# The order of 16 small matmuls in a linear-attention and MLP kernel: two batches by turns, or one after the other

## Chip, cores and metric

The kernel runs on 1 core of one Trainium2 chip. The metric is the device time of the execution in microseconds (us), as the median of several runs. The profile is taken by the hardware profiler from one execution of its own.

## What is computed

Inputs are q, k, v of shape (8 batches, 8 heads, 576 positions, 64) and two weight matrices, 512 x 2048 and 2048 x 512, in float32. For each batch and head:

```
phi(x) = [relu(x) * cos(w), relu(x) * sin(w)]      # 128 features, w by position
kv  = phi(k)^T v          (128 x 64)      z = sum over positions of phi(k)
num = phi(q) kv           (576 x 64)      den = phi(q) z + 1e-06
x   = num / den           -> 4608 tokens x 512
out = relu(x @ w_in)^2 @ w_out            -> 4608 x 512
```

## The kernel before, in words

Everything runs in bfloat16 on TensorE with sums in PSUM. The kernel has two parts that it weaves together: the attention of batch b, and the MLP of batches before it. The MLP's products mostly use a Strassen-like scheme with seven products in place of eight (the tiles ha, hb, hc, ya, yb, yc), and plain products near the start (hps, yh).

A batch has 576 positions: four blocks of 128 and a rest of 64. For each block the numerator (`num_div`, L685) takes 8 matmuls, one a head: the turned query features of the block (`qpT`, 128 features x 128 positions) are the stationary operand, loaded by a weight load, and the head's 65 columns of `kvz` (kv and z side by side, so numerator and denominator come out together) are the moving one. The result, 128 positions x 65 columns a head, goes to the tile `num`: two PSUM banks, four heads in each.

The rests of 64 positions of two successive batches b-1 and b (b odd) are taken together, once a pair. Rows 0 to 63 of `num` are for batch b-1, rows 64 to 127 for batch b (`sides`, by b % 2). This is `mm_num` with j == J (L599), which calls `mm_num_tail` (L610) for the one batch and then for the other. Each call issues 8 matmuls, one a head, whose stationary operand is 128 features x 64 positions. They fill half of the array's columns: 0 to 63 for batch b-1 and 64 to 127 for batch b. The loops run over `hh` (four heads) and `half` (which of the two banks). All 16 are first and last of their sums: nothing accumulates. The turned features of a pair's rests lie in one tile, `qpTt`.

One division by DVE (`div`, L642) then serves both batches: it adds a small constant to the denominators (L627), takes the reciprocal (L628) and multiplies (L633), into `xpt`. There are four such groups of 16, for the pairs (0, 1), (2, 3), (4, 5) and (6, 7). What they yield is turned by a transpose and used by the last step of the MLP (`G8` and `Y8`), which handles the rests of all batches.

The order of work is written out by hand. `Plan` holds operations with their dependencies, and `ORDER` (L23) lists all of them by name; `Plan.run` (L221) walks the list, picks the buffer of each tile with estimated times and emits the instructions, so each engine executes its operations in the order of that list. The four groups are its entries num1.4, num3.4, num5.4 and num7.4, each one indivisible operation for the plan, with an estimated time of 0.5 us on TensorE. Each stands far behind num1.3, num3.3 and so on, the other numerators of the later batch, which read the same `kvz`. All matmuls are issued by `mm` (L460), so the profile shows them under L461; they are told apart by tiles: the 16 of a group are `num<-kvz,qpTt`, and the weight loads (PEld) `<-qpTt`. The other numerators are `num<-kvz,qpT`.

Of the kernel before, what the change touches and what calls it, by code (L numbers as in the profile page):

```python
# [282 lines left out]
def kernel(  # L283
# [13 lines left out]
    E1 = D + 1  # L297
# [6 lines left out]
    HH = H // 2  # L304
# [98 lines left out]
    sides = [slice(g * TAIL, (g + 1) * TAIL) for g in range(2)]  # L403
# [56 lines left out]
    def mm(out, lhsT, rhs, start, stop=True):  # L460
        nc.tensor.matmul(  # L461
            out=out, lhsT=lhsT, rhs=rhs, start=start, stop=stop, skip_group_check=True
        )
# [5 lines left out]
    vs, kq, kqt, fe, fet, kz, kvz, qpT, qpTt = {}, {}, {}, {}, {}, {}, {}, {}, {}  # L469
# [128 lines left out]

    def mm_num(num, b, j):  # L599
        if j == J:  # L600
            for i in range(2):
                mm_num_tail(num, b - 1 + i)
            return
        for hh in range(HH):
            for half in range(2):
                e0, h = hh * E1, half * HH + hh
                o, lhsT = num[half][:, e0 : e0 + E1], qpT[b, j // 2][:, j % 2, h, :]
                mm(o, lhsT, kvz[b][:, h * E1 : (h + 1) * E1], True)

    def mm_num_tail(num, b):  # L610
        for hh in range(HH):
            for half in range(2):
                e0, h, s_ = hh * E1, half * HH + hh, sides[b % 2]
                o = num[half][s_, e0 : e0 + E1]
                lhsT = old_turned(b)[:, hh, sides[half]] if b < 2 else qpTt[b][:, h, s_]
                mm(o, lhsT, kvz[b][:, h * E1 : (h + 1) * E1], True)

    def old_turned(b):
        return qpTt[b][:, b * HH : (b + 1) * HH, :]
# [65 lines left out]
    def num_div(b, j, after, bufs):  # L685
        num = buf("n", [P, 2, FP], F32, "num")
        den = buf("den", [P, 2, 2, HH], F32, "den")
        xbuf = xp[b, j // 2] if j < J else xpt[b]
        n = plan.op(
            f"num{b}.{j}",  # L690
            {"PE": 0.244 if j < J else 0.5},
            lambda e: mm_num([num[:, 0], num[:, 1]], b, j),
            after,
            [num, kvz[b], den, xbuf] + bufs,
        )
        return plan.op(
            f"div{b}.{j}",
            {"DVE": 0.99},
            lambda e: div(num[:, :], b, j, den),
            [n],  # L700
            [num, den, xbuf],
        )
# [919 lines left out]
```

## Time and profile before

| | us |
|---|---|
| median of 3 runs | 272.38 |
| lowest and highest | 271.87, 273.05 |
| the profiled execution, its own time | 271.95 |
| its span, first to last instruction | 269.9 |
| matmuls (PE) busy in it | 263.1 |
| weight loads (PEld) busy | 225.0 |
| DVE, ACT busy | 228.1, 186.7 |

PE is TensorE's matmuls and PEld its weight loads, which overlap with matmuls. Each group of 16 stands in the profile as 16 instructions with 65 columns each (128 features in, 64 positions out). The length given for one instruction (0.19 to 0.22 us here) is the time until it has passed the array; the next one starts well before that, so what an instruction costs is read from the distances between starts. A view by windows counts the instructions that touch a window; if all windows begin before the group, the count is how many have started by the window's end.

### The profile page before, as it was taken

The page shows a single profiled execution, that of the slowest core. Times are in us where ns is not written, and L with a number is a line of the kernel's source. Part 1 is how long each engine was busy: PE and PEld are TensorE (multiplying, and loading weights), DVE is VectorE, ACT ScalarE, POOL GpSimd, SP SyncE. Part 2 cuts the span into 40 slices and gives each one's busy share as a digit, 9 for nine tenths or more (in the row PEclk, how much of TensorE's full clock was granted, in tenths as well). Part 3 has the DMA queues.
Part 4 walks back from the last instruction along what each step waited for, and adds up shares of the span by engine and source line. Part 5 has one row for each costly group of instructions (what it writes and reads, how often), then busy time and mean ns, then how long its engine had stood idle before and what let it go on. Part 6 is the DMA issues. An engine that isn't in the chain of part 4 may idle for free.

```text
span 269.9 us, 6751 instructions
## 1 busy us (share of the span) xinstructions
PE 263.1 (97%) x2787; PEld 225.0 (83%) x2792; DVE 228.1 (85%) x412; ACT 186.7 (69%) x289; POOL 26.9 (10%) x44
## 2 busy tenths in 40 slices
PE   8899999999999999999999999999999999999994
PEld 3568856699899889989998998899888888888883
DVE  3877987889998999999999999899978858797941
ACT  4762695698888997689699868587658636755510
POOL 8934443200000000000000000000000000000000
PEclk9999999999999999999999999999999999999999
DMA  6999999999899999999899998652540111010115
GB/s 221 220 206 253 328 198 250 298 295 298 221 247 314 221 261 298 300 183 231 284 275 209 232 359 208 152 155 100 61 125 15 38 63 78 8 72 2 78 50 186
DMA packets 82367, 51.23 MB, mean 190 GB/s; under 512 B 53217, under 2 KB 78817, under 8 KB 82337
## 3 DMA queue, kind: packets, MB, share of 16 engines
q1 hardware_dynamic: 71008, 38.28, 55.5%
q0 software_dynamic: 10736, 12.00, 21.2%
q10 hardware_dynamic: 592, 0.52, 0.6%
q8 instruction: 22, 0.36, 0.6%
q14 instruction: 9, 0.07, 0.1%
HBM read 36.70 MB, written 9.44 MB: 171 GB/s over the span
## 4 chain that ended last, share of the span: by engine, by line
PE 83%; DMA 12%; POOL 3%; issue 0%; DVE 0%; POOLq 0%
PE ya L461 18%; PE yb L461 16%; PE hb L461 13%; PE ha L461 8%; PE hc L461 8%; PE hps L461 8%; DMA w1sb<-in_moe_w_in_dram 5%; DMA kq<-in_k_dram 4%; PE num L461 3%; DMA w2sb<-in_moe_w_out_dram 3%; PE kz L461 3%; PE yc L461 3%; PE yh L461 3%; POOL kq L509 1%; POOL w1sb L411 1%; POOL v L1378 1%
## 5 line engine op out<-in xcount | busy, mean ns | idle before, releaser
L461 PEld LDWEIGHTS <-w1sb 128*128 128x128 bf16 x736 | 70.4, 98 | 8.6
L461 PEld LDWEIGHTS <-gs 128*128 128x128 bf16 x512 | 49.9, 98 | 5.8
L461 PEld LDWEIGHTS <-gT 128*128 128x128 bf16 x448 | 43.1, 98 | 9.8 <-issue 0.2
L442 ACT ACTIVATE gT<-gT 128x1024 bf16<-128x1024 bf16 x38 | 39.5, 1059 | 3.4 <-DVE gT L455 1.8
L461 PE MATMUL hps<-xT,w1sb 128*128 128x256 bf16 x320 | 37.4, 273 | 0.0
L448 ACT ACTIVATE fe<-kq,cols 128x1024 bf16<-128x1024 f32 (+1 forms) x39 | 35.1, 950 | 2.8 <-DMA kq<-in_k_dram 1.7
L461 PEld LDWEIGHTS <-w1s 128*128 128x128 bf16 x312 | 29.7, 98 | 3.3
L461 PE MATMUL ya<-w2sb,gT 128*128 128x256 bf16 x256 | 30.7, 273 | 0.0
L461 PE MATMUL hb<-xs,w1sb 128*128 128x256 bf16 x208 | 30.6, 273 | 0.0
L450 DVE TENSOR_SCALAR fe<-kq,cols 128x1024 bf16<-128x1024 f32 (+1 forms) x41 | 26.9, 690 | 4.0 <-DMA kq<-in_k_dram 4.0
L461 PE MATMUL ha<-xT,w1sb 128*128 128x256 bf16 x176 | 26.2, 273 | 0.0
L444 DVE TENSOR_TENSOR gT<-gT 128x1024 bf16<-128x1024 bf16 x34 | 23.2, 686 | 1.2 <-ACT gT L436 0.8
L436 ACT ACTIVATE gT<-ha 128x512 bf16<-128x512 f32 x21 | 12.6, 601 | 15.9 <-PE ha L461 15.9
L633 DVE TENSOR_TENSOR xp<-num,den 128x512 bf16<-128x512 f32 (+1 forms) x33 | 22.2, 675 | 1.1
L436 ACT ACTIVATE gT<-hps 128x512 bf16<-128x512 f32 x26 | 15.4, 602 | 8.1 <-PE hps L461 8.0
L455 DVE CUSTOM_DVE_ANT_0 gT<-hb,s 128x512 bf16<-128x512 f32 x26 | 17.8, 686 | 3.7 <-PE hb L461 3.3
L458 DVE TENSOR_TENSOR gs<-gT 128x2048 bf16<-128x2048 bf16 x16 | 19.4, 1219 | 0.4
L455 DVE CUSTOM_DVE_ANT_0 gT<-hc,u 128x512 bf16<-128x512 f32 x26 | 17.7, 683 | 0.8 <-PE hc L461 0.8
L432 ACT COPY hb<-ha 128x512 f32<-128x512 f32 x26 | 15.2, 585 | 4.3 <-DVE gT L438 1.8
L461 PE MATMUL hb<-xs,w1s 128*128 128x256 bf16 x104 | 15.6, 273 | 0.0
L436 ACT ACTIVATE gT<-hb 128x512 bf16<-128x512 f32 x18 | 10.8, 599 | 7.0 <-PE hb L461 4.5
L461 PE MATMUL hc<-xs,w1s 128*128 128x256 bf16 x104 | 15.6, 273 | 0.0
(120 smaller groups left out, 415.7 us busy)
## 6 DMA issues: line engine op xcount, KB each, us to landing
out_dram<-y SPq DMA_DIRECT2D x16, 512.0 KB, 3.7
vs<-in_v_dram SPq DMA_DIRECT2D x10, 512.0 KB, 4.8
kq<-in_k_dram SPq DMA_DIRECT2D x5, 1024.0 KB, 7.1
kq<-in_q_dram SPq DMA_DIRECT2D x5, 1024.0 KB, 9.2
w1sb<-in_moe_w_in_dram POOLq DMA_DIRECT2D x4, 512.0 KB, 11.6
w2sb<-in_moe_w_out_dram POOLq DMA_DIRECT2D x4, 512.0 KB, 10.3
kq<-in_q_dram POOLq DMA_DIRECT2D x2, 1024.0 KB, 11.2
kq<-in_k_dram POOLq DMA_DIRECT2D x2, 1024.0 KB, 11.1
```

What stands on the lines that cost most here:

```text
L411: nc.gpsimd.dma_start(out=w1sb[:, :, f0:f1], in_=moe_w_in[:, f0:f1].rearrange("(kb p) f -> p kb f", p=P),)
L432: (nc.scalar.copy if e == "ACT" else nc.vector.tensor_copy)(out=out, in_=in_)
L436: nc.scalar.activation(out=out, in_=in_, func=ACTF.Relu)
L442: nc.scalar.activation(out=out, in_=in_, func=ACTF.Square)
L444: nc.vector.tensor_tensor(out=out, in0=in_, in1=in_, op=ALU.mult)
L448: nc.scalar.activation(out=out, in_=in_, func=ACTF.Relu, scale=col)
L450: nc.vector.tensor_scalar(out=out, in0=in_, scalar1=0.0, scalar2=col, op0=ALU.max, op1=ALU.mult)
L455: nc.vector._custom_dve(dve_ops.TENSOR_ADD_SAT, out=out, in0=in0, in1=in1, s0=BIG, s1=0.0)
L458: nc.vector.tensor_tensor(out=out, in0=in0, in1=in1, op=op)
L461: nc.tensor.matmul(out=out, lhsT=lhsT, rhs=rhs, start=start, stop=stop, skip_group_check=True)
L509: eng.dma_start(out=kq[b][:, "kq".index(nm)][:, hs, js], in_=main_of(nm, b)[:, hs, js])
L633: nc.vector.tensor_tensor(out=x, in0=n4[:, :, :, 0:D].rearrange("p b (k l) d -> p b k l d", l=2), in1=r.rearrange("p b (k l) -> p b k l", l=2)
```

## The change

The 16 matmuls of a group are issued in another order. Before: all 8 of batch b-1, then all 8 of batch b. After: for each head and bank, the one of batch b-1 and then the one of batch b. `mm_num_tail` becomes the body of the loops, with `hh` and `half` as arguments. Operands, results, and everything else of the kernel are the same, as is `ORDER`.

```diff
     def mm_num(num, b, j):
         if j == J:
-            for i in range(2):
-                mm_num_tail(num, b - 1 + i)
+            for hh in range(HH):
+                for half in range(2):
+                    for i in range(2):
+                        mm_num_tail(num, b - 1 + i, hh, half)
             return
...
-    def mm_num_tail(num, b):
-        for hh in range(HH):
-            for half in range(2):
-                e0, h, s_ = hh * E1, half * HH + hh, sides[b % 2]
-                o = num[half][s_, e0 : e0 + E1]
-                lhsT = old_turned(b)[:, hh, sides[half]] if b < 2 else qpTt[b][:, h, s_]
-                mm(o, lhsT, kvz[b][:, h * E1 : (h + 1) * E1], True)
+    def mm_num_tail(num, b, hh, half):
+        e0, h, s_ = hh * E1, half * HH + hh, sides[b % 2]
+        o = num[half][s_, e0 : e0 + E1]
+        lhsT = old_turned(b)[:, hh, sides[half]] if b < 2 else qpTt[b][:, h, s_]
+        mm(o, lhsT, kvz[b][:, h * E1 : (h + 1) * E1], True)
```

## Prediction

> **What bounds the kernel now.** I read the page first: busy times, the chain that ended last, then the waits of TensorE. From the page:
>
> ```profile
> PE 263.1 (97%) x2787; PEld 225.0 (83%) x2792; DVE 228.1 (85%) x412; ACT 186.7 (69%) x289; POOL 26.9 (10%) x44
> PEclk9999999999999999999999999999999999999999
> PE 83%; DMA 12%; POOL 3%; issue 0%; DVE 0%; POOLq 0%
> ```
>
> TensorE (PE) is busy 97% of a span of 269.9 us at full clock, and it is 83% of the chain that ended last. The 16-matmul bursts that change run at 73, 94, 170 and 210 us, so what counts is whether PE is the bound from 73 us to the end. Two views answer that. The first is the table of busy time by stretch (us of the stretch's length, then busy us and number of instructions of each engine):
>
> ```profile
> 73.00:94.00 21.00, 21.00 (x258) 18.82 (x256) 19.30 (x38) 18.76 (x28) 0.00 (x0) 1.00 1.04 251
> 94.00:170.00 76.00, 76.00 (x865) 68.34 (x864) 73.60 (x133) 63.11 (x97) 0.00 (x0) 1.00 1.06 258
> 170.00:211.00 41.00, 41.00 (x450) 36.82 (x451) 35.62 (x63) 27.17 (x42) 0.00 (x0) 1.00 0.38 91
> 211.00:264.00 53.00, 53.00 (x487) 47.43 (x486) 40.22 (x58) 27.31 (x44) 0.00 (x0) 1.00 0.15 53
> ```
>
> PE's busy time equals the length of each stretch. The second is the view of waits: all of PE's own, then those of its weight loads from 50 to 265 us, then the longest of all engines from 73.6 to 260 us (first and fourth of that answer).
>
> ```profile
> PE wm L461 <- DVE zeros L362: 1.2, 1, 1.2
> PE tq L1428 <- DVE fe L450: 0.7, 1, 0.7
> PE num L461 <- ACT kvz L432: 0.2, 1, 0.2
> ```
> ```profile
> PEld L461 <- issue: 0.8, 4, 0.2
> ```
> ```profile
> ACT gT L436 <- PE ha L461: 15.9, 11, 3.5
> ...
> ACT u L432 <- PE hb L461: 3.6, 7, 1.0
> ```
>
> PE's three waits belong to the warm-up and the first batch. In the stretch that matters its weight loads stand still 4 times for 0.2 us, and on nothing that the profile names: those are the starts of the four bursts. The other engines wait for PE, not the reverse. So in this stretch every tenth of a microsecond that PE is spared should come off the end, and every tenth that it is given should be added.
>
> **What the bursts cost now.** Of each burst, the chart of instructions in order of time (start, length, engine, work, count) shows the burst and what follows. All four, each from its own answer:
>
> ```profile
> 72.59 0.60 PE L461 MATMUL yc<-w2t,gs 128*128 128x256 bf16 x4
> 73.12 0.60 PE L461 MATMUL num<-kvz,qpTt 128*64 128x65 bf16 x16
> 73.65 0.61 PE L461 MATMUL yb<-w2t,gs 128*128 128x256 bf16 x4
> ```
> ```profile
> 94.14 0.60 PE L461 MATMUL num<-kvz,qpTt 128*64 128x65 bf16 x16
> 94.67 0.50 PE L461 MATMUL ya<-w2sb,gT 128*128 128x256 bf16 x3
> ```
> ```profile
> 169.90 0.60 PE L461 MATMUL num<-kvz,qpTt 128*64 128x65 bf16 x16
> 170.43 0.61 PE L461 MATMUL hb<-xs,w1sb 128*128 128x256 bf16 x4
> ```
> ```profile
> 210.27 0.60 PE L461 MATMUL num<-kvz,qpTt 128*64 128x65 bf16 x16
> 210.80 0.61 PE L461 MATMUL hb<-xs,w1sb 128*128 128x256 bf16 x4
> ```
>
> From the first matmul of a burst to the first of the next work it is 0.53 us in all four. The inside of a burst is read from windows that all begin at 73.10 and end later and later: the count behind PE is how many of the 16 have started by then, the count behind PEld how many weight loads have.
>
> ```profile
> 73.10:73.13 0.03, 0.01 (x1) 0.01 (x1) 0.00 (x0) 0.00 (x0) 1.00 0.00 0
> 73.10:73.17 0.07, 0.05 (x1) 0.05 (x2) 0.00 (x0) 0.00 (x0) 1.00 0.56 59
> 73.10:73.18 0.08, 0.06 (x2) 0.06 (x3) 0.00 (x0) 0.00 (x0) 1.00 0.49 51
> 73.10:73.26 0.16, 0.14 (x4) 0.14 (x5) 0.00 (x0) 0.00 (x0) 1.00 0.30 45
> 73.10:73.27 0.17, 0.15 (x5) 0.15 (x5) 0.00 (x0) 0.00 (x0) 1.00 0.29 42
> 73.10:73.28 0.18, 0.16 (x6) 0.16 (x7) 0.00 (x0) 0.00 (x0) 1.00 0.45 51
> 73.10:73.33 0.23, 0.21 (x8) 0.21 (x9) 0.00 (x0) 0.00 (x0) 1.00 0.37 45
> 73.10:73.34 0.24, 0.22 (x9) 0.22 (x11) 0.00 (x0) 0.00 (x0) 1.00 0.35 43
> 73.10:73.36 0.26, 0.24 (x9) 0.24 (x11) 0.00 (x0) 0.00 (x0) 1.00 0.41 51
> 73.10:73.37 0.27, 0.25 (x11) 0.25 (x12) 0.00 (x0) 0.00 (x0) 1.00 0.47 53
> 73.10:73.51 0.41, 0.39 (x15) 0.39 (x16) 0.00 (x0) 0.00 (x0) 1.00 0.50 77
> 73.10:73.53 0.43, 0.41 (x16) 0.41 (x16) 0.00 (x0) 0.00 (x0) 1.00 0.49 79
> ```
>
> The first start is at 73.12, the second just after 73.17 and the sixteenth at about 73.52: 0.40 us for 15 gaps. They are not even. Four or five starts come by 73.27, about one in 0.03 us or a little more; between 73.27 and 73.37 there are six; then five take the last 0.16 us. The fifth and the sixth stand just before and just after 73.27, and the tenth and the eleventh both fall into the 10 ns before 73.37. I read this as two streams. Compare a burst of eight full-width matmuls with the same 65 columns, counted in the same way:
>
> ```profile
> 83.38:83.40 0.02, 0.01 (x1) 0.00 (x0) 1.00 0.57 205
> 83.38:83.61 0.23, 0.23 (x8) 0.00 (x0) 1.00 1.05 374
> ```
>
> Seven gaps in some 0.21 us make 0.03 us each: one stream takes 65 columns every 0.03 us, so starts that coincide must be in different halves of the array. The first eight of a burst fill columns 0 to 63 of the array (the earlier batch, result rows 0 to 63), the second eight columns 64 to 127. The second half's stream began with the sixth start, at about 73.275, while the first half's ended at about 73.365; each then needs 0.245 us for its eight (73.12 to 73.365, and 73.275 to 73.52). They overlap for 0.09 us only, because the second stream's first pair is the ninth in program order and was taken up 0.155 us after the first.
>
> **The change part by part.** It removes no instruction and adds none. In the lists of instructions in program order both kernels have 5586 entries on PE, and DVE, ACT, POOL and SP have the same entries in the same order; within each burst the same 16 pairs of weight load and matmul stand in turn, one for the earlier batch and one for the later. The first pair keeps the only two waits of the burst and no wait is added. The values of the later batch that now come second instead of ninth (its kvz) had been read by that batch's own numerators long before.
>
> What moves is the start of the second stream. Its first pair is now the second one handed out. In the rows above, eight pairs were handed out before the ninth began, in 0.155 us, so handing out takes at most 0.02 us a pair. With a stream length of 0.245 us the sixteenth start comes 0.245 + 0.02 = 0.265 us after the first, against 0.40: **0.135 us less a burst**. Bounds on both sides: if the second stream loses nothing, 0.25 and a gain of 0.15; if handing out at 0.02 us a pair is itself the limit, 15 x 0.02 = 0.30 and a gain of 0.10. I take 0.135, between them, since the 0.02 is itself only an upper bound.
>
> Four bursts give 4 x 0.135 = **0.54 us** (0.40 to 0.60). The pause before a burst (73.12 follows the previous matmul by 0.2 us) and the 0.13 us from its last start to the next work lie outside the 16 and stay. As PE waits for nobody afterwards, the gain goes through to the last matmul; what follows that, the last copies and stores up to 269.9 us, hangs on PE and moves with it. DVE's division behind a burst starts no later than now.
>
> The sum against the profiled execution's own time: that was 271.95 us (span 269.9 and 2.05 around it), so 271.95 - 0.54 = 271.41. The runs shown have a median of 272.38, 0.43 above it, from 271.87 to 273.05. For the median I forecast 272.38 - 0.54 = 271.84, say **271.8 us**, 0.2% less. About 0.5% (1.36 us) is what a measurement of this kernel can tell from no change, so this counts as within it.
>
> A rule that speaks against the change: the Trainium skill, page "TensorE: Matmul & The Clock Gate", section "The mechanism" (of its Part 3), says that weight loads overlap with matmuls in flight only when their row groups differ. Both halves here use all 128 rows, so by it the streams could not run beside each other, and nothing would be gained. The trace does not agree: between 73.27 and 73.28 two weight loads start (5 to 7) beside matmuls whose rows last 0.19 us and more.
>
> **The rivals.**
>
> *Handing out is the limit.* The 16 starts average 0.40 / 15 = 0.0267 us, and that may be a floor on starts rather than an accident of two streams. Then the order doesn't matter, the gain is nil and the time 272.4. For it: the average is close to a single stream's 0.03. Against it: the five starts between 73.26 and 73.34 come every 0.016 us, and six in the 0.10 us up to 73.37, so the floor would have to let a backlog through. The same page of the Trainium skill, section "Wait — 56ns, not 53.3ns?", has a floor of 25 ns from start to start however small the matmul; an estimate from it is 15 x 0.025 = 0.375 us a burst, 0.1 us in all, 272.3. The trace's starts within 10 ns of each other don't agree.
>
> *The gain is taken back on PE.* PE then reaches later waits up to 0.54 us early. Where a product is held by DVE or ACT, PE would stand still instead. DVE is busy 73.60 of 76.00 us from 94 to 170, the tightest stretch, so part of the gain of the first two bursts (0.27) could go: 271.8 + 0.27 = 272.1, at worst 272.4. Against it: those engines' waits are on PE and would shift with it, and no wait on an input transfer appears among the waits from 73.6 to 260 us.
>
> *Each turn to the other half costs.* A stream that is taken up afresh starts slowly: the second start of the burst comes some 0.05 us after the first, and in the second stream, if I read it rightly, its first and second (sixth and ninth of all) are 0.06 us apart, where 0.03 is usual. If that price was paid at every change of half, 15 gaps of 0.05 to 0.06 us make 0.75 to 0.90 us in place of 0.40, or 4 x 0.35 to 4 x 0.50 = 1.4 to 2.0 us: 273.8 to 274.4, slower. It decides as soon as the mean gap is over 0.0267 us. Against it: in the overlap the array already goes back and forth between the halves (starts within 10 ns), and the gaps there are shorter, not longer.
>
> That the change does not do what it says is ruled out by the order of the instructions.
>
> **How the numbers follow.** Chances: the forecast 0.70, handing out 0.13, taken back 0.10, a price for each turn 0.07. Only the last lies outside 0.5%. The scatter of the runs before (0.5 below and 0.7 above their median) is as large as the effect: 271.84 - 0.5 = 271.3 at the low end, 271.2 with the bound of 0.60; at the high end the cases without gain (272.4) with part of that scatter, 272.7. Left out above are the price for each turn and the far scatter. Range 271.2 to 272.7. Faster by over 0.5% would need 1.36 us, 0.34 of the 0.40 us in every burst, which no case gives: 0.02 for scatter. Slower by over 0.5%: 0.06. Within: 0.92.
>
> **What would show it.** In the changed profile: 0.39 to 0.40 us from the first matmul of a burst to the first of the next work, not 0.53, in all four; starts in pairs from the beginning, two in 0.03 us; the burst at 210 us some 0.4 us earlier than now and the span some 0.5 us shorter. A burst still 0.53 long speaks for the limit on handing out, one of 0.9 to 1.0 for the price for each turn; short bursts with an unchanged span, and new idle time of PE in the waits, for the gain taken back.

## The result, and the profile after

The changed kernel takes 271.58 us (median of 22 runs, 271.0 to 272.83), the kernel before 272.49 in the same series (22 runs, 271.74 to 274.07). The ratio is 0.9967, 95% interval 0.9954 to 0.998: 0.9 us less, by the interval 0.5 to 1.25. A second series below gives 0.9994. The forecast was 271.8, 0.54 less. So the sign is right, and what is left to settle is how much of the 0.9 is the change.

The bursts first. In the profile after, the chart of TensorE (PE) in order of time shows (start, length, work, count), for each burst and what follows:

```profile
72.89 0.44 PE L461 MATMUL num<-kvz,qpTt 128*64 128x65 bf16 x16
73.26 0.94 PE L461 MATMUL yb<-w2t,gs 128*128 128x256 bf16 x7
...
93.83 0.44 PE L461 MATMUL num<-kvz,qpTt 128*64 128x65 bf16 x16
94.21 0.61 PE L461 MATMUL ya<-w2sb,gT 128*128 128x256 bf16 x4
...
169.58 0.44 PE L461 MATMUL num<-kvz,qpTt 128*64 128x65 bf16 x16
169.95 0.61 PE L461 MATMUL hb<-xs,w1sb 128*128 128x256 bf16 x4
...
209.79 0.44 PE L461 MATMUL num<-kvz,qpTt 128*64 128x65 bf16 x16
210.17 0.61 PE L461 MATMUL hb<-xs,w1sb 128*128 128x256 bf16 x4
```

From a burst's first matmul to the next work it is 0.37 or 0.38 us where it was 0.53, four times alike: 0.376 by the trace's nanoseconds, 0.153 less each and 0.61 in all. Inside the first burst, by windows that all begin at 72.87 and whose counts are the starts so far:

```profile
72.87:72.90 0.03, 0.01 (x2) 0.01 (x2) 0.00 (x0) 0.00 (x0) 1.00 0.57 137
72.87:72.93 0.06, 0.04 (x2) 0.04 (x4) 0.00 (x0) 0.00 (x0) 1.00 0.39 102
72.87:72.95 0.08, 0.06 (x4) 0.07 (x6) 0.00 (x0) 0.00 (x0) 1.00 0.37 102
72.87:73.00 0.13, 0.11 (x6) 0.12 (x8) 0.00 (x0) 0.00 (x0) 1.00 0.40 118
72.87:73.12 0.25, 0.23 (x14) 0.23 (x16) 0.00 (x0) 0.00 (x0) 1.00 0.44 135
72.87:73.14 0.27, 0.25 (x16) 0.26 (x16) 0.00 (x0) 0.00 (x0) 1.00 0.42 133
```

The counts grow by twos. In nanoseconds the starts are 0 and 4, 53 and 56, 89 and 92, and so on to 244 and 248: two streams of eight beside each other from the beginning, and each keeps the pace that one had alone. (A trace doesn't say to which half a start belongs. It is read from the distances: in one stream the starts of these bursts are at least 0.029 us apart.)

Now the span: 269.3 us against 269.9. The first burst begins at 72.89, 0.23 us earlier than in the profile before, and nothing ahead of it was changed. So a fairer measure runs from the first burst to the last block of 16 matmuls, which begins at 264.14 in the profile before:

```profile
262.83 1.47 PE L461 MATMUL yb<-w2t,gT 128*128 128x256 bf16 x12
264.14 1.91 PE L461 MATMUL ya<-w2sb,gT 128*128 128x256 bf16 x16
```

and in the profile after:

```profile
262.75 0.93 PE L461 MATMUL yb<-w2t,gT 128*128 128x256 bf16 x7
263.51 1.91 PE L461 MATMUL ya<-w2sb,gT 128*128 128x256 bf16 x16
```

264.14 - 73.12 = 191.02 us before, 263.51 - 72.89 = 190.62 after: **0.40 less, not 0.61**. I call this the stretch below. The missing 0.21 is in two new waits of PE. The view of waits of PE's weight loads from 60 to 265 us now has a second line:

```profile
PEld L461 <- issue: 0.8, 4, 0.2
PEld L461 <- DVE gT L455: 0.3, 1, 0.3
```

The chart after, around 98 us and around 77 us:

```profile
97.56 0.68 DVE L455 CUSTOM_DVE_ANT_0 gT<-hc,u 128x512 bf16<-128x512 f32 x1
97.73 1.06 ACT L442 ACTIVATE gT<-gT 128x1024 bf16<-128x1024 bf16 x1 [0.28 <-DVE gT L438]
98.16 0.74 DVE L450 TENSOR_SCALAR fe<-kq,cols 128x1024 bf16<-128x1024 f32 x1
98.29 0.22 PEld L461 LDWEIGHTS <-w1sb 128*128 128x128 bf16 x3 [0.26 <-DVE gT L455]
98.29 0.39 PE L461 MATMUL ha<-xT,w1sb 128*128 128x256 bf16 x2
```
```profile
76.11 0.68 DVE L432 COPY yu<-yb 128x512 f32<-128x512 f32 x1
76.66 0.39 PEld L461 LDWEIGHTS <-gs 128*128 128x128 bf16 x3
76.71 0.74 DVE L450 TENSOR_SCALAR fe<-kq,cols 128x1024 bf16<-128x1024 f32 x1
76.84 0.38 PE L461 MATMUL yb<-w2sb,gs 128*128 128x256 bf16 x2
```

At 98.29 PE has waited 0.14 us longer than the usual distance for DVE's sum of hc and u, which ends at 97.56 + 0.68 = 98.24; at 76.84 it has waited 0.08 for the copy yu, which ends at 76.79. In both places PE goes on 0.05 us after DVE's end. The second does not even show in the view of waits: it is read from the distance to the matmul before, 0.189 us where 0.109 is usual. The same two operations stood close to PE already in the profile before:

```profile
97.86 0.68 DVE L455 CUSTOM_DVE_ANT_0 gT<-hc,u 128x512 bf16<-128x512 f32 x1
...
98.46 0.74 DVE L450 TENSOR_SCALAR fe<-kq,cols 128x1024 bf16<-128x1024 f32 x1
98.60 0.33 PEld L461 LDWEIGHTS <-w1sb 128*128 128x128 bf16 x4
```
```profile
76.34 0.68 DVE L432 COPY yu<-yb 128x512 f32<-128x512 f32 x1
...
77.15 0.27 PE L461 MATMUL yb<-w2sb,gs 128*128 128x256 bf16 x1
```

They ended at 98.54 and 77.02, and what needs them on PE, the weight load and the matmul yb, came at 98.60 and 77.15: 0.06 and 0.13 us later. Of that, 0.05 us pass even where PE stands waiting. So PE had next to nothing in hand at the sum and some 0.07 us at the copy, while it was to come 0.15 us earlier behind each burst. That fits the losses of 0.14 and 0.08.

### The profile page after: what moved, and what is told of

The parts are those of the page before. It is cut to its first block, busy times and chain, and to the rows that moved or that the text cites. A ratio compares the mean times of both kernels' runs of the same rounds, so it can differ in the third digit from the quotient of the medians.

```text
span 269.3 us, 6756 instructions
## 1 busy us (share of the span) xinstructions
PE 263.3 (98%) x2792; PEld 224.4 (83%) x2792; DVE 228.7 (85%) x412; ACT 187.1 (69%) x289; POOL 26.8 (10%) x44
## 4 chain that ended last, share of the span: by engine, by line
PE 93%; DVE 2%; DMA 2%; issue 0%; ACT 0%; SPq 0%
PE ya L461 18%; PE yb L461 16%; PE hps L461 13%; PE hb L461 13%; PE ha L461 9%; PE hc L461 8%; PE yh L461 5%; PE num L461 4%; PE kz L461 3%; PE yc L461 3%; DMA kq<-in_k_dram 2%; PE tq L651 1%; DVE fe L450 1%; PE tx L656 1%; DVE xp L633 0%
## 5 line engine op out<-in xcount | busy, mean ns | idle before, releaser
L461 PE MATMUL yh<-w2sb,gT 128*128 128x512 bf16 x64 | 15.4, 379 | 0.0
```

What stands on the lines that cost most here:

```text
L461: nc.tensor.matmul(out=out, lhsT=lhsT, rhs=rhs, start=start, stop=stop, skip_group_check=True)
```

## The experiments

The theory after the result: two streams run beside each other, 0.153 us a burst; 0.22 of the 0.61 is lost to DVE behind the first two bursts; the rest of the timed 0.9 us lies ahead of the first burst and is chance. The main rival: the timed ratio holds something else of the change.

**e1: the changed kernel again**, with no edit.

> The changed kernel once more, against the kernel before on the same chip. Theory A, only the bursts count: each of the four is 0.15 us shorter, 0.61 in all, less 0.22 for two new waits of TensorE (at 77 and 98 us) gives 0.39 us, a ratio of 0.9986. Theory B, the timed ratio of 0.9967 holds more than the bursts: about 0.9 us again. In the trace both expect 0.376 us from the start of a burst to the next work, and the two new waits. The first burst's start, 0.23 us earlier in the one profile so far, is chance if it comes elsewhere now, within some 0.3 us of 73.0.

272.01 us (12 runs) against 272.1 (23 runs), ratio 0.9994, interval 0.998 to 1.0008. That holds 0.9986 and leaves out 0.9967. The chart:

```profile
73.14 0.44 PE L461 MATMUL num<-kvz,qpTt 128*64 128x65 bf16 x16
...
263.76 1.91 PE L461 MATMUL ya<-w2sb,gT 128*128 128x256 bf16 x16
```

The first burst is at 73.14, not 72.89: its place was chance. The stretch is 190.62 again, to the hundredth. So two profiles of one kernel agree in the stretch to 0.01 us, and the whole time scatters far more: over the twelve profiles taken, the first burst begins anywhere from 72.75 to 74.15 us. What the change is worth behind the first burst is 0.40 us, a ratio of 0.9985. The second series' interval holds that and the first's leaves it out (it ends at 0.998). That the surplus of the first series is the scatter of the start is argued from the profiles, not shown: those runs have no profiles.

**e2 and e3: the bursts four times over**, apart and by turns.

```diff
-            for hh in range(HH):
-                for half in range(2):
-                    for i in range(2):
-                        mm_num_tail(num, b - 1 + i, hh, half)
+            for i in range(2):                 # e2; in e3 the loop over i is the innermost
+                for again in range(4):
+                    for hh in range(HH):
+                        for half in range(2):
+                            mm_num_tail(num, b - 1 + i, hh, half)
```

> Each burst's 8 matmuls of the earlier batch four times over, then the 8 of the later batch four times over: 32 and 32, the same results written again. Two streams, one for each half of the array: 31 gaps of 0.032 and the slow first one make 1.01 us a stream, the second begins some 0.09 before the first ends, so 1.93 to the last start and 2.06 us to the next work; 1.53 more than before a burst, 6.1 us in all, ratio 1.0225. If starts are limited by handing out at 0.0267 us: 63 x 0.0267 + 0.13 = 1.81 us, 5.1 us in all.

> The 16 by turns, four times over, the same results written again. Two streams beside each other throughout: 1.01 to the last start, 1.14 us to the next work, 0.61 more than before a burst, 2.4 us in all, ratio 1.009; 3.7 us less than the 32 and 32. If only the first few starts of a burst can be packed and handing out then limits at 0.0267 us: 1.81 us, the same as 32 and 32.

In e2:

```profile
72.75 2.12 PE L461 MATMUL num<-kvz,qpTt 128*64 128x65 bf16 x64
74.81 1.37 PE L461 MATMUL yb<-w2t,gs 128*128 128x256 bf16 x11
...
269.85 1.91 PE L461 MATMUL ya<-w2sb,gT 128*128 128x256 bf16 x16
```

In e3:

```profile
73.65 1.21 PE L461 MATMUL num<-kvz,qpTt 128*64 128x65 bf16 x64
74.79 1.48 PE L461 MATMUL yb<-w2t,gs 128*128 128x256 bf16 x12
...
267.10 1.91 PE L461 MATMUL ya<-w2sb,gT 128*128 128x256 bf16 x16
```

A burst takes 2.06 us apart and 1.14 by turns, as worked out from two streams; 64 starts by turns in 1.01 us are one every 16 ns, so a floor of 0.0267 us on starts is out. The stretch is 197.10 and 193.45 us: 6.08 and 2.43 more than before, as expected. Timed, e2 is 277.64 (ratio 1.0198, interval 1.0181 to 1.0214, which leaves out the 1.0225 expected) and e3 274.88 (1.0091, 1.0073 to 1.0109), from 4 runs each. The 2.8 us between them is clear of the noise, as the two intervals lie apart: matmuls by turns save time in the whole run, not in the trace only. It is 0.9 less than the 3.65 between the stretches. In the two profiles the first burst begins at 72.75 and 73.65 us, which is as much; that the other runs differ in the same way is not shown.

**e5 and e6: two and two, four and four by turns.** What had held the second stream back for 0.155 us?

```diff
+            heads = [(hh, half) for hh in range(HH) for half in range(2)]
+            for at in range(0, H, 4):          # e6; 2 in e5
+                for i in range(2):
+                    for hh, half in heads[at : at + 4]:
+                        mm_num_tail(num, b - 1 + i, hh, half)
```

> Two matmuls of one batch, two of the other, and so on. What set the 0.155 us after which the second stream began in the kernel before? Theory W, a short window: the later half's first pair is taken up once about five instructions or fewer of the other half wait ahead of it (there: matmul 6, loads and matmuls 7 and 8). With two pairs ahead only a load and a matmul wait, so it starts about 0.003 us after the first, as by single turns; the burst is 0.38 us to the next work. Theory H, handing out at 0.0195 us a pair: it starts 0.039 us after, and the burst is about 0.41.

> Four and four by turns. Theory W: six instructions wait ahead at first, five once the second load has started at 0.027, so the later half starts some 0.03 us after the first; 0.40 us to the next work. Theory H: 4 x 0.0195 = 0.078 us after; 0.45 to the next work.

By twos the other half starts 0.006 us after the first and the burst is 0.379 us to the next work; by fours it starts 0.013 after, by the windows of e6:

```profile
73.35:73.37 0.02, 0.01 (x1) 0.01 (x1) 0.00 (x0) 0.00 (x0) 1.00 0.00 0
73.35:73.38 0.03, 0.02 (x2) 0.02 (x2) 0.00 (x0) 0.00 (x0) 1.00 0.10 34
```

and the burst is 0.401. Theory H (0.039 and 0.078) falls: handing out takes 3 ns a pair, not 20. Theory W gave 0.38 and 0.40 rightly and missed the start by fours (0.03 expected): six instructions waiting ahead, three pairs, do not hold the other half back yet. With that number the kernel before fits, where the second stream did not begin behind the fourth matmul of the first (four pairs still waiting) but 6 ns after the fifth (pairs 6, 7 and 8 still waiting), and e2 as well, by its windows:

```profile
72.74:73.60 0.86, 0.85 (x26) 0.85 (x27) 0.00 (x0) 0.00 (x0) 1.00 0.58 99
72.74:73.65 0.91, 0.90 (x28) 0.90 (x29) 0.00 (x0) 0.00 (x0) 1.00 0.59 107
72.74:73.68 0.94, 0.93 (x30) 0.93 (x31) 0.00 (x0) 0.00 (x0) 1.00 0.61 114
```

28 starts at their even pace, then two within 0.03 us, 6 ns apart in the trace: the 29th of the first half and the first of the other, again with three pairs waiting. Whether the limit is one of instructions or of pairs these runs don't tell. (e5 to e9 were run once each, in 271.2 to 273.0 us, which is too few for effects of this size; they count here by their traces alone.)

**e7: the other PSUM bank.**

```diff
-                        mm_num_tail(num, b - 1 + i, hh, half)
+                        mm_num_tail(num, b - 1 + i, hh, half if i == 0 else 1 - half)
```

> By turns, but the later batch takes the heads of the other PSUM bank first, so that the two halves of the array never write one bank at one time. Theory: the halves don't disturb each other in one bank, and the burst stays 0.376 us to the next work. Rival: part of the 0.03 us a gap, or of the slow first gap of 0.053, is the shared bank; then the burst is shorter, by up to 8 x 0.003 = 0.02 us if the gaps fall to the 0.029 of the smallest.

0.376 or 0.377 us in all four bursts, and a stretch of 263.52 - 72.91 = 190.61. Sharing a bank costs the two halves nothing that these traces show.

**e8 and e9: by turns in the first two bursts only, in the last two only** (a condition on b, the old loops otherwise).

> By turns in the bursts at 73 and 94 us alone. Theory: the two new waits of TensorE (0.08 and 0.14 us) come from being early behind these two bursts, so they are here too, and from the first burst's start to the end of the span it is 196.8 - 0.30 + 0.22 = 196.7 us. Rival: the waits belong to the profiled execution and not to the change; then they are gone, and it is 196.5.

> By turns in the bursts at 170 and 210 us alone. Theory: no product behind these two bursts stands close enough to VectorE to wait, so the whole gain of 2 x 0.153 goes through: from the first weight load of the first burst to the last weight load of the kernel 192.55 - 0.31 = 192.25 us (192.55 before, 192.15 to 192.16 with all four), and no new wait. Rival: being early costs behind these bursts too, as behind the first two (0.22 of 0.31 lost): 192.45.

In e8, and then in e9:

```profile
74.15 0.44 PE L461 MATMUL num<-kvz,qpTt 128*64 128x65 bf16 x16
...
265.07 1.91 PE L461 MATMUL ya<-w2sb,gT 128*128 128x256 bf16 x16
```
```profile
73.40 0.60 PE L461 MATMUL num<-kvz,qpTt 128*64 128x65 bf16 x16
...
264.12 1.91 PE L461 MATMUL ya<-w2sb,gT 128*128 128x256 bf16 x16
```

The stretch is 190.92 in e8, 0.10 less than before, with both new waits; 190.72 in e9, 0.30 less, with none. So the gain of the last two bursts goes through whole, and two thirds of that of the first two are lost to DVE. The parts add up: 0.10 + 0.30 = 0.40. The kernel before has one profile only, but e9 keeps its order up to the third burst and repeats its pace there: 170.19 - 73.40 = 96.79 us from the first burst to the third, against 169.90 - 73.12 = 96.78.

**e4 and e10: another order on DVE.** In the list of work, Y1.u2 is the copy yu, G2.3.c12r the sum of hc and u, G2.3.c21r the relu of hb, div1.4 the division of the first pair, and sin and cos are the feature operations (in e10 div1.4 leaves its old place behind Y1.P7):

```diff
-sin3.2 xTd2.1 num1.4 cos3.3* Y1.P6 H2.1.10.0 Y1.u2 H2.0.11.0 ...
+xTd2.1 num1.4 cos3.3* Y1.P6 H2.1.10.0 Y1.u2 sin3.2 H2.0.11.0 ...               # e4
+xTd2.1 num1.4 cos3.3* Y1.P6 H2.1.10.0 Y1.u2 div1.4 sin3.2 H2.0.11.0 ...        # e10
...
-G2.2.c12r sin4.0 cos4.1* cos4.2* G2.3.P4 G2.3.c21r xTd3.1 ldv5.2 G2.3.c12r sin4.2
+G2.2.c12r sin4.0 cos4.1* cos4.2* G2.3.c12r G2.3.P4 G2.3.c21r xTd3.1 ldv5.2 sin4.2   # e4
+G2.2.c12r G2.3.c12r cos4.1* cos4.2* G2.3.P4 G2.3.c21r sin4.0 xTd3.1 ldv5.2 sin4.2   # e10
```

> The changed kernel with two moves in the order of work on VectorE: the copy yu one feature operation earlier (76 us), the sum of hc and u ahead of the relu of hb (98 us). Theory: the two new waits of TensorE, 0.08 and 0.14 us, are VectorE finishing these two late, and go. Then from the first burst's start to the end of the span it is 196.2 us against 196.4 in the changed kernel and 196.8 before, ratio 0.9977. Rival: VectorE is simply full there (73.60 of 76 us busy), and the waits come back elsewhere: 196.4.

> The changed kernel with another order on VectorE alone: behind the copy yu (76 us) the division of the first pair comes next, ahead of two feature operations; at 96 us the sum of hc and u takes the place of a feature operation, which goes behind the relu of hb, so that the relu, whose delay cost 0.6 us in e4, stays where it was. Theory: the new waits at 77 and 98 us go and none takes their place: first burst's first weight load to the last weight load 192.15 - 0.22 = 191.93 us; timed ratio to the kernel before 0.998 if the first 73 us come out alike. Rival: VectorE is full there and a wait comes back further on, in the products that need the delayed features: 192.15 or more.

e4 took 272.5 us (ratio 1.001, 0.9997 to 1.0022) and its stretch is 264.58 - 73.53 = 191.05 us, 0.43 more than in the changed kernel. The two waits are gone, but the relu of hb, now behind the sum, feeds a square on ACT, and PE stands still for that instead. The waits of PE, and then of its weight loads, in e4 from 73.6 to 260 us:

```profile
PE ya L461 <- ACT gT L442: 0.3, 1, 0.3
```
```profile
PEld L461 <- issue: 0.8, 4, 0.2
PEld L461 <- ACT gT L442: 0.5, 1, 0.5
```

So the expectation's rival, a wait that comes back elsewhere, was right there, and the wait cost more than the rival said. e10 leaves the relu in its place and lets the feature operations, which nobody needs soon, go last:

```profile
73.30 0.44 PE L461 MATMUL num<-kvz,qpTt 128*64 128x65 bf16 x16
...
263.61 1.91 PE L461 MATMUL ya<-w2sb,gT 128*128 128x256 bf16 x16
```

Its stretch is 190.31, 0.31 less than in the changed kernel and 0.71 less than before: more than the 0.22 expected, because an older wait of 0.09 us at 93 us went too. DVE was not full; its order was unlucky. Timed it is 272.35 (12 runs, 271.06 to 273.74) against 272.31 (17 runs), ratio 0.9997, interval 0.9975 to 1.002; 0.71 us less would be 0.9974, just outside it. By the stretch, in one profile, it is the best version; that it is faster in the whole time is not shown.

## Why the prediction was right, point by point

- *PE is the bound from 73 us on, so what it is spared comes off the end.* Right for the last two bursts (e9), and only a third right for the first two (e8). The table of busy time, 76.00 of 76.00 us, could not show it: waits of 0.1 us between matmuls do not appear there, and the profile after still shows the same 76.00. What hints at it in the profile before are the two groups of rows above, where PE follows DVE's end by 0.06 and 0.13 us only.
- *Two streams, 0.245 us each.* Right. e2, e3 and the starts in pairs show it.
- *Handing out takes up to 0.02 us a pair, so 0.135 a burst.* This term was mis-sized: 3 ns a pair, and 0.153 a burst, a little past the upper bound of 0.15. The 0.155 us that I read as eight handings-out was a short window over waiting instructions (e5, e6).
- *Sum 0.54 us.* The bursts gave 0.61, the two waits took 0.22, the stretch is 0.40 shorter: the low end of the term. The timed 0.9 of the first series was above it and the 0.2 of the second (1 - 0.9994 of 272.1) below; 0.40 lies between them. How near the forecast came is partly luck: of the first series' 0.9 only 0.40 is seen in the stretch, and in the sum the gain of a burst was taken too small while the loss to the waits was left out.
- *Rivals.* The floor on starts is out (e3, one start in 16 ns), and with it, for matmuls in two halves of the array, the 25 ns of the Trainium skill's page "TensorE: Matmul & The Clock Gate", section "Wait — 56ns, not 53.3ns?". The price for each turn is out: the two starts of a pair are 3 or 4 ns apart. The reading that its price came from is off too: by the nanoseconds the second stream's first two starts are the sixth and the eighth of the burst, not the sixth and the ninth, and 0.052 us apart as in the first stream. The rule of the Trainium skill, same page, section "The mechanism", that weight loads overlap with running matmuls only in another row group does not hold for two column halves: in the windows after, four loads and two matmuls have started by 72.93. "The gain is taken back" came true for a third of the gain, by the mechanism that it named (DVE, the first two bursts), with a chance of 0.10.

## What to carry to other kernels

Matmuls that fill half of the array's columns are worth issuing by turns between the halves: here the engine found work for the other half behind three waiting pairs of the first, and not behind four or more (the kernel before, e2, e6). When an engine that is never idle is made faster, look at who finishes just ahead of it, in pairs of rows, before crediting the gain: two products with some 0.07 us and next to nothing in hand took a third of it. And to measure an effect smaller than the scatter, compare the stretch behind the part that scatters.

## What the runs showed of the hardware

The two halves keep their full pace beside each other, 65 columns every 0.03 us in each, whether they write one PSUM bank (the changed kernel) or two (e7). The second matmul of a fresh stream comes 0.052 to 0.054 us after its first in every burst, whether the other half is at work or not, and the later ones every 0.03 us. And a burst of half-width matmuls has a price at its edges that the order does not touch: the first start comes some 0.202 us after the matmul before it where 0.109 is usual, and the next full-width matmul some 0.128 us after the last one where 0.03 is, in all bursts before and after. Eight full-width matmuls of the same 65 columns pay neither: at 139.87 us in the profile before they start 0.109 us after the matmul ahead of them, and the next work 0.029 us after the last. What the price consists of no run here shows.
